# Order of two first loads on the ACT queue, and the length of TensorE's fillers, in a gated attention and mixer kernel

## The chip, the cores and the metric

The kernel runs on one core of a Trainium2 chip. The metric is the device time of one execution in microseconds (us). Medians are of all executions of a kernel, and runs count as "fast" where nothing put them over 1.5% above the fastest of the same kernel. The whole kernel takes about 267 us, and the change is about the first 7 of them, so everything below is about tenths of a microsecond.

## The reference

```python
def reference(A_x, A_wqkv, A_wo, B_x, B_w1, B_w2, B_w3, B_w4, gate_w):
    x = A_x                                            # 1 x 2048 x 640, bf16
    g = sigmoid((x * gate_w).sum(-1, keepdims=True))   # one gate per row
    a = A_ref(x, A_wqkv, A_wo)                         # linear attention, 32 heads
    b = B_ref(x, B_w1, B_w2, B_w3, B_w4)               # mixer block and MLP
    return g * a + (1 - g) * b
# A_ref begins with qkv = x @ wqkv; the kernel starts with the k part of it.
# ... the rest is not touched by the change
```

## The kernel before

It starts with k = x @ wk, for 16 chunks of 128 rows. The product needs x transposed. Chunk 0 is loaded as it is (`load_x(0, 1)`), transposed by TensorE against an identity matrix and copied from PSUM by VectorE. The other chunks come through loads that transpose (`load_xT`), all on the sync queue. The 640 x 640 matrix wk comes in five pieces of 128 rows (`load_wk`), of 160 KB each. The gate vector is transposed too and becomes one more column of wk, so that the gate's logits fall out of the same products.

```python
    sp, aq, gq = nc.sync, nc.scalar, nc.gpsimd
    # load_x, load_xT: on sp.  load_wk(q, dc): rows dc*128 to dc*128+127 of wk, on queue q
    load_x(0, 1)
    aq.dma_start(g5[:], gate_w.rearrange("(c p) -> c p", p=P))
    load_wk(sp, 1)
    load_wk(aq, 0)
    load_wk(aq, 2)
    load_wk(sp, 3)
    load_wk(aq, 4)
    for c0, c1 in ((1, 2), (2, 3), (3, 4), (4, 6), (6, 8), (8, 12), (12, 16)):
        load_xT(c0, c1)
    # ... the other loads
    def warmup(n, w=TS):                      # TS = 512: fillers, their result is never read
        for i in range(n):
            nc.tensor.matmul(warm[:, 1, 0:w], lhsT=one[:, 0:P], rhs=one[:, 0:w], start=True, stop=True)

    warmup(6)
    warmup(3, P)                              # P = 128
    # ... tiles
    for n, (ptb, a, b) in enumerate(turns):   # ((0, 2), (2, 5)): five transposes in two groups
        for dc in range(a, b):
            nc.tensor.transpose(ptb[...], x_sb[:, 0, dc * P:(dc + 1) * P], ident[:])
        nc.vector.tensor_copy(xT[:, a:b, 0:P], ptb[...])
        if n == 0:
            nc.tensor.transpose(tg[:, 0:DC], g5[:], ident[0:DC, 0:DC])
            nc.vector.tensor_copy(wk_sb[:, :, D], tg[:, 0:DC])
    warmup(3, P)
    for dc in range(DC):                      # chunk 0, piece by piece as wk lands
        k_mm(kp, 0, (dc,))
        if dc < DC - 1:
            warmup(1, 2 * P)
    k_evac(kp, 0)
    for c in range(1, NCH):                   # chunks 1 to 15
        pt = pair()
        k_mm(pt, c, range(DC))
        k_evac(pt, c)
```

Of the kernel before, what the change touches and what calls it, by code (L numbers as in the profile page):

```python
# [16 lines left out]
def kernel(  # L17
# [14 lines left out]
    P = 128  # L32
# [36 lines left out]
    def pair():  # L69
        return ps.tile([P, 2, 512], F32, name="pp")  # L70
# [44 lines left out]
    sp, aq, gq = nc.sync, nc.scalar, nc.gpsimd  # L115

    def load_x(c0, c1):
        sp.dma_start(x_sb[:, c0:c1, 0:D], x2[c0 * P:c1 * P, :].rearrange("(c p) d -> p c d", p=P))
# [4 lines left out]
    def load_wk(q, dc):  # L123
        q.dma_start(wk_sb[:, dc, 0:D], A_wqkv[dc * P:(dc + 1) * P, D:2 * D])  # L124

    load_x(0, 1)
    aq.dma_start(g5[:], gate_w.rearrange("(c p) -> c p", p=P))
    load_wk(sp, 1)
    load_wk(aq, 0)
    load_wk(aq, 2)  # L130
    load_wk(sp, 3)
    load_wk(aq, 4)
# [67 lines left out]
    def warmup(n, w=TS):  # L200
        for i in range(n):
            nc.tensor.matmul(warm[:, 1, 0:w], lhsT=one[:, 0:P], rhs=one[:, 0:w], start=True, stop=True)

    warmup(6)
    warmup(3, P)
    kp = pair()
    turns = [(pair()[:, 0, :].bitcast(BF16), a, b) for a, b in ((0, 2), (2, DC))]
    tg = warm[:, 0, :].bitcast(BF16)
# [387 lines left out]
```

## Time and profile before

| | before |
|---|---|
| median | 266.91 us of 3 (266.3, 266.91 and one of 305.26) |
| span of the profiled execution | 264.4 us |
| TensorE busy | 259.7 us, 98% |
| first x chunk lands | 3.08 us |
| transposes start | 3.66 us |
| first product with wk | 4.73 us |
| chunk 1 starts | 6.57 us |
| transposed chunks 8 to 11 land | 16.29 us |
| chunk 8 starts | 16.34 us |

Times in such tables are counted from the span's start. Landings and starts of single matmuls come from the trace. L190 is the line of the k products, L202 of the fillers, L211 and L214 of the transposes, L121 of the transposing loads, L118 of plain x loads, L124 of the wk pieces.

Busy times of the kernel before, from the page: engine, us, share of the span, instructions.

```profile
PE 259.7 (98%) x1744; PEld 162.2 (61%) x1744; DVE 139.3 (53%) x270; ACT 85.1 (32%) x126; POOL 20.2 (8%) x55
```

TensorE bounds the kernel as a whole. But the chain of waits of the first 30 us of the kernel before (start us, us, what) does not run through TensorE until 16.3 us:

```profile
0.79 0.40 SPq L118
...
2.18 1.29 SPq L121
...
3.52 1.27 SPq L121
...
9.35 6.94 DMA xT<-in_A_x_dram
16.29 0.05 issue
16.34 11.07 PE pp L190 x80
```

SPq is the sync queue, which issues one load after another; a transposing load holds it for over 1.2 us. The sixth one, of chunks 8 to 11, is issued at 9.35 us and lands 6.94 us later. TensorE begins chunk 8 only then.

The k products of the kernel before, and what TensorE's weight loads waited for (us, times):

```profile
L190 PE MATMUL pp<-wk_sb,xT x160: 296/300/310, 4.7 to 27.1; 128*128 128x320 bf16 x80, 128*128 128x321 bf16 x80
...
  DMA xT<-in_A_x_dram: 0.6, 2
```

The three numbers are the least, median and greatest duration in ns: no product is slow. A chunk takes ten of them, 1.36 us. With chunk 1 at 6.57 us and no wait, chunk 8 would start at 6.57 + 9.54 = 16.11 us (9.54 is the distance of these two starts when TensorE doesn't wait). It started at 16.34, so about 0.23 us were spent waiting. That is the slack behind the start.

TensorE in the start of the kernel before, from the timeline (start us, us, engine, line, operation):

```profile
2.92 0.95 PE L202 MATMUL pp<-const-bfloat16-1.0 128*128 128x512 bf16 x4
3.66 0.42 PE L211 MATMUL pp<-ident,x_sb 128*128 128x128 bf16 x2
4.01 0.18 PE L214 MATMUL pp<-ident,g 5*128 5x5 bf16 x1
4.13 0.36 PE L211 MATMUL pp<-ident,x_sb 128*128 128x128 bf16 x3
4.55 0.33 PE L202 MATMUL pp<-const-bfloat16-1.0 128*128 128x128 bf16 x3
4.73 0.43 PE L190 MATMUL pp<-wk_sb,xT 128*128 128x320 bf16 x2
```

The first x load and its time to landing, kernel before:

```profile
L118 SPq DMA_DIRECT2D x_sb<-in_A_x_dram x1: 402/402/402, 0.8 to 0.8; - x1
...
DMA to landing us min/median/max: 2.3/2.3/2.3
```

Piece 0 of wk, second on the ACT queue, landed at 4.68 us and its first product started at 4.73. So piece 0 looks like what held chunk 0 back. But the last of the three short fillers ahead of that product began at 4.67 us, 0.06 us before it, so this trace alone can't tell whether chunk 0 waited for the piece or for TensorE itself.

### The profile page before, as it was taken

The page shows a single profiled execution, that of the slowest core. Times are in us where ns is not written, and L with a number is a line of the kernel's source. Part 1 is how long each engine was busy: PE and PEld are TensorE (multiplying, and loading weights), DVE is VectorE, ACT ScalarE, POOL GpSimd, SP SyncE. Part 2 cuts the span into 40 slices and gives each one's busy share as a digit, 9 for nine tenths or more (in the row PEclk, how much of TensorE's full clock was granted, in tenths as well). Part 3 has the DMA queues.
Part 4 walks back from the last instruction along what each step waited for, and adds up shares of the span by engine and source line. Part 5 has one row for each costly group of instructions (what it writes and reads, how often), then busy time and mean ns, then how long its engine had stood idle before and what let it go on. Part 6 is the DMA issues. An engine that isn't in the chain of part 4 may idle for free.

```text
span 264.4 us, 4255 instructions
## 1 busy us (share of the span) xinstructions
PE 259.7 (98%) x1744; PEld 162.2 (61%) x1744; DVE 139.3 (53%) x270; ACT 85.1 (32%) x126; POOL 20.2 (8%) x55
## 2 busy tenths in 40 slices
PE   8999999999999999999999999999999999999994
PEld 4767555788755644555667555667565667455762
DVE  1788688899858588955403464503455313112132
ACT  1555444321165636622502212312131422233000
POOL 7100010012300140001000001000001000000000
PEclk9999999999999999999999999999999999999999
DMA  7999978015673727600132000042000041100011
GB/s 202 184 211 365 377 222 318 0 43 121 128 92 68 78 51 193 207 0 2 25 74 77 25 0 2 0 99 75 26 0 2 1 99 58 44 0 2 0 59 40
DMA packets 46093, 23.61 MB, mean 89 GB/s; under 512 B 35451, under 2 KB 45435, under 8 KB 46075
## 3 DMA queue, kind: packets, MB, share of 16 engines
q1 hardware_dynamic: 45632, 22.86, 34.0%
q10 hardware_dynamic: 442, 0.49, 0.5%
q8 instruction: 13, 0.21, 0.3%
q14 instruction: 6, 0.04, 0.1%
HBM read 12.21 MB, written 2.62 MB: 56 GB/s over the span
## 4 chain that ended last, share of the span: by engine, by line
PE 91%; SPq 3%; DMA 3%; ACT 1%; issue 0%; DVE 0%
PE pp L479 22%; PE pp L460 21%; PE pp L307 8%; PE pp L413 8%; PE pp L444 8%; PE pp L341 8%; PE pp L232 8%; PE pp L190 4%; SPq L121 3%; DMA xT<-in_A_x_dram 3%; PE pp L468 1%; PE pp L488 1%; ACT m_sb L381 1%; PE pp L360 1%; PE pp L247 0%; SPq L124 0%
## 5 line engine op out<-in xcount | busy, mean ns | idle before, releaser
L460 PE MATMUL pp<-lnxT,w_sb 128*128 128x512 bf16 x260 | 60.4, 379 | 0.0
L479 PE MATMUL pp<-w_sb,h 128*128 128x256 bf16 (+1 forms) x416 | 57.9, 299 | 0.0
L462 ACT ACTIVATE h<-pp 128x1024 bf16<-128x1024 f32 (+1 forms) x28 | 26.9, 961 | 82.2 <-PE pp L460 82.2
L479 PEld LDWEIGHTS <-h 128*128 128x128 bf16 x416 | 40.3, 98 | 16.6 <-issue 1.1
L460 PEld LDWEIGHTS <-w_sb 128*128 128x128 bf16 x260 | 25.4, 98 | 26.8
L495 DVE SCALAR_TENSOR_TENSOR oc<-pp,omg,x 128x640 bf16<-128x640 f32 x15 | 12.9, 882 | 44.0 <-ACT h2x L471 21.3
L447 DVE SCALAR_TENSOR_TENSOR x<-pp,gate,x 128x640 f32<-128x640 f32 x16 | 13.9, 868 | 29.4 <-PE pp L444 29.4
L416 DVE TENSOR_TENSOR x<-pp,x_sb 128x640 f32<-128x640 f32 x16 | 13.1, 820 | 22.6 <-PE pp L413 22.6
L182 ACT ACTIVATE e<-pp 128x640 bf16<-128x640 f32 (+1 forms) x26 | 21.5, 826 | 9.6 <-PE pp L232 9.6
L444 PE MATMUL pp<-m_sb,pqT 128*128 128x320 bf16 x160 | 24.3, 299 | 0.0
L413 PE MATMUL pp<-w_sb,hsT 128*128 128x320 bf16 x160 | 23.9, 299 | 0.1
L190 PE MATMUL pp<-wk_sb,xT 128*128 128x320 bf16 (+1 forms) x160 | 22.6, 300 | 0.1
L307 PE MATMUL pp<-x_sb,pk 128*128 128x320 bf16 (+1 forms) x160 | 22.3, 300 | 0.0
L232 PE MATMUL pp<-xT,hsT 128*128 128x512 bf16 x100 | 21.7, 379 | 0.0
L307 PEld LDWEIGHTS <-pk 128*128 128x128 bf16 x160 | 18.8, 117 | 3.5
L413 PEld LDWEIGHTS <-hsT 128*128 128x128 bf16 x160 | 15.6, 98 | 8.2 <-issue 0.2
L444 PEld LDWEIGHTS <-pqT 128*128 128x128 bf16 x160 | 15.7, 98 | 7.7
L190 PEld LDWEIGHTS <-xT 128*128 128x128 bf16 x160 | 15.4, 98 | 6.4 <-DMA xT<-in_A_x_dram 0.6
L341 PE MATMUL pp<-lnxT,w_sb 128*128 128x512 bf16 x80 | 17.9, 379 | 0.0
L232 PEld LDWEIGHTS <-hsT 128*128 128x128 bf16 x100 | 11.8, 118 | 9.7
L277 POOL TENSOR_SCALAR rstd<-mv 128x4 f32<-128x4 f32 (+1 forms) x11 | 3.4, 313 | 156.5 <-DVE mv L283 156.5
L184 DVE SCALAR_TENSOR_TENSOR pk<-pp,e 128x640 bf16<-128x640 f32 x16 | 13.2, 825 | 1.7
(77 smaller groups left out, 191.6 us busy)
## 6 DMA issues: line engine op xcount, KB each, us to landing
out_dram<-oc SPq DMA_DIRECT2D x15, 160.0 KB, 1.8
w_sb<-in_B_w_dram SPq DMA_DIRECT2D x1, 2160.0 KB, 8.4
w_sb<-in_B_w_dram SPq DMA_DIRECT2D x1, 2080.0 KB, 10.0
x_sb<-in_A_x_dram SPq DMA_DIRECT2D x2, 640.0 KB, 10.7
x_sb<-in_A_x_dram SPq DMA_DIRECT2D x1, 1120.0 KB, 8.2
wo_sb<-in_A_wo_dram SPq DMA_DIRECT2D x6, 160.0 KB, 8.3
hsT<-in_A_wqkv_dram SPq DMA_DIRECT2D x1, 800.0 KB, 5.7
m_sb<-in_A_wqkv_dram SPq DMA_DIRECT2D x1, 800.0 KB, 11.5
```

The costliest lines, as they stand in the source:

```text
L182: nc.scalar.activation(ev, src, ACT.Exp)
L184: nc.vector.scalar_tensor_tensor(dst, src, 0.0, ev, op0=ALU.max, op1=ALU.add)
L190: nc.tensor.matmul(pt[:, hf, 0:n], lhsT=xT[:, dc, c * P:(c + 1) * P], rhs=wk_sb[:, dc, hf * HD:hf * HD + n], start=(dc == 0), stop=(dc == ...
L232: nc.tensor.matmul(pt[:, t % 2, :], lhsT=wq_sb[:, dc, :].rearrange("p (m j) -> p j m", j=DC)[:, j], rhs=xT[:, dc, t * TS:(t + 1) * TS], st ...
L307: nc.tensor.matmul(pt[:, hf, 0:HD + hf], lhsT=w, rhs=x_sb[:, c, hf * HD:(hf + 1) * HD + hf], start=(c == 0), stop=(c == NCH - 1))
L341: nc.tensor.matmul(pt[:, i, :], lhsT=w, rhs=lnxT[t][:, dc, :], start=(dc == 0), stop=(dc == DC - 1))
L413: nc.tensor.matmul(pt[:, hf, 0:HD], lhsT=hsT[:, fc, 2 + c * P:2 + (c + 1) * P], rhs=w2_sb[:, fc, hf * HD:(hf + 1) * HD], start=(fc == 0), ...
L444: nc.tensor.matmul(pt[:, hf, 0:HD], lhsT=pqT[:, j, c * P:(c + 1) * P], rhs=m_sb[:, j, hf * HD:(hf + 1) * HD], start=(j == 0), stop=(j == D ...
L447: nc.vector.scalar_tensor_tensor(x1, pt[:, :, 0:HD], gate[:, c:c + 1], x1, op0=ALU.mult, op1=ALU.add)
L460: nc.tensor.matmul(pt[:, k, :], lhsT=w3_sb[:, dc, fc * P:(fc + 1) * P], rhs=lnT[:, dc, :], start=(dc == 0), stop=(dc == DC - 1))
L462: nc.scalar.activation(h2[:, 2 * i * TS:(2 * i + n) * TS], pt[:].rearrange("p h e -> p (h e)")[:, 0:n * TS], ACT.Gelu_apprx_tanh)
L479: nc.tensor.matmul(dst, lhsT=st[t]["h2"][:, fc * TS + cc * P:fc * TS + (cc + 1) * P], rhs=w4_sb[:, fc, a:b], start=start and fc == 0, stop ...
```

## The change

Its intent: piece 0 is wanted first of all pieces, so it goes first on its queue, and the gate vector second. The fillers are lengthened to keep TensorE at work until x is there.

```diff
     load_x(0, 1)
+    load_wk(aq, 0)
+    load_wk(sp, 1)
     aq.dma_start(g5[:], gate_w.rearrange("(c p) -> c p", p=P))
-    load_wk(sp, 1)
-    load_wk(aq, 0)
     load_wk(aq, 2)
@@
-    warmup(6)
-    warmup(3, P)
+    warmup(7)
+    warmup(1, P)
```

One more thing moves that the diff doesn't show. Eight semaphores serve the loads of the sync and ACT queues in turn (numbers 100 and 102 to 108 in the traces of both kernels). The second transposing load shares its semaphore with the first load on the ACT queue: the gate vector before, piece 0 after.

## The prediction

> **What bounds the kernel now.** TensorE: the busy table gives PE 259.7 us of a 264.4 us span (98%). The change touches only the first 7 us, and there the chain of waits does not run through PE: from 0.79 to 16.29 us it follows the sync queue, which issues the first x load, two wk pieces and then seven transposing loads of x, one after another at 1.27 to 3.56 us each. It leaves that queue with the landing of transposed chunks 8 to 11 at 16.29 us; PE takes over at 16.34. Reading the matmuls one by one, chunk 7 has streamed out by about 16.12, so PE stands still some 0.22 us there: the slack behind the start.
>
> **The start, from the timeline.** Six 512-wide fillers run from 0.83 us, 0.427 us apart [...]; three 128-wide ones (0.107 us each) end at 3.66. The first x chunk landed at 3.08, so its transposes begin only when the fillers end. The gate vector, first on the ACT queue (0.57 us to issue), landed at 2.14, long before its use at 4.01. Wk piece 0, second there, landed at 4.68, and its first product started at 4.73, just as the last short filler ended. Chunk 0 runs to 6.54 us; chunk 1 starts at 6.57, when its transposed x has landed (6.52).
>
> **What the change does.** It removes two 128-wide fillers and adds one 512-wide: 0.427 - 0.213 = +0.21 us ahead of the transposes, which begin near 3.88. Wk piece 0 is issued at 0.79 instead of 1.39, so it should land 0.6 to 1 us earlier, near 3.7 to 4.1. It now starts beside the first x load. [...] I expect x to land near 3.4 to 3.9 (this trace shows x alone, 2.3 us to landing, the other pieces at 3.3 to 3.9). The gate vector lands near 2.6 to 4, perhaps just in time. So chunk 0 starts at about 4.9 and ends near 6.7.
>
> **A side effect.** The second transposing load on the sync queue waits for the semaphore of the first DMA on the ACT queue. That was the gate vector's (2.14; no wait, the load was issued at 3.52). Now it is wk piece 0's. If that lands after 3.5, the transposing loads, which are on the chain, slip by 0 to 0.5 us; I guess 0.2.
>
> **On the critical path.** PE being 0.15 to 0.2 us later at the start is swallowed by the 0.22 us wait at chunk 8. An earlier wk piece 0 buys nothing there either. The slip of the transposing loads would pass on in full. Sum: 0 to +0.5 us, middle +0.1 us, of 266.9.
>
> **Prediction:** 267.0 us, 8 in 10 between 266.1 and 268.0. Faster by over 2%: 0.01; within 2%: 0.97; slower by over 2%: 0.02.
>
> **What would show it.** Right: the chain of waits still enters PE at chunk 8, near 16.3 to 16.6 us, behind the transposing load; wk piece 0 lands before 4.2; x lands after 3.3; later stages keep their lengths. Wrong: chunk 8 starts below 16.2, or PE waits for x or the gate vector for over 0.3 us.
>
> **What would make it wrong.** The full clock was granted at 4.2 us[...]. A faster landing of the transposing loads could gain up to 0.2 us, as much as PE waits for them.

Three passages are cut from the text, and the cuts are marked, because no trace or run shows what they said: a word on the clock of the fillers (the trace has no clock record before 4.2 us), a reason for the later landing of x, and the length and cost of a later full clock. None was a term of the sum, which came to 0 to +0.5 us, middle +0.1 us, on 266.9 us: the later clock was named as a risk beside it.

## The result, and the profile after

The changed kernel took 266.87 us in the median of 4 executions (266.47 to 266.91). The kernel before stood at 266.7 us in the median of 4 by then, one of them the 305.26. The ratio of the fast runs was 1.0008, with a 95% interval of 0.9988 to 1.0028: the same. Ratios here are the mean time of one kernel's fast runs over that of the other's of the same rounds, so not quite the ratio of the medians quoted.

The first trace after the change looks quite different from the one before, for a change of nothing. Busy times of the changed kernel, from the page:

```profile
PE 260.5 (98%) x1743; PEld 162.8 (61%) x1743; DVE 139.3 (53%) x270; ACT 85.1 (32%) x126; POOL 20.3 (8%) x55
```

Its chain of waits in the first 30 us:

```profile
0.83 3.25 PE pp L202 x8
...
5.24 0.54 PE pp L190 x2
...
6.66 0.27 PE pp L190 x2
...
7.42 20.71 PE pp L190 x152
```

Here the chain is TensorE from the first filler on. The same pair of k products takes 0.54 us at 5.24 and 0.27 us at 6.66: at 5.24 us TensorE took twice as long for the same work. The trace's clock records begin with the full clock at 6.445 us, against 4.205 us in the trace before. The k products say the same, and that nothing was waited for (the list of waits is empty):

```profile
L190 PE MATMUL pp<-wk_sb,xT x160: 299/300/475, 5.0 to 27.8; 128*128 128x320 bf16 x80, 128*128 128x321 bf16 x80
```

TensorE in the start, from the timeline of the changed kernel:

```profile
3.88 0.42 PE L211 MATMUL pp<-ident,x_sb 128*128 128x128 bf16 x2
4.23 0.18 PE L214 MATMUL pp<-ident,g 5*128 5x5 bf16 x1
4.34 0.50 PE L211 MATMUL pp<-ident,x_sb 128*128 128x128 bf16 x3
4.76 0.48 PE L202 MATMUL pp<-const-bfloat16-1.0 128*128 128x128 bf16 x3
5.04 0.74 PE L190 MATMUL pp<-wk_sb,xT 128*128 128x320 bf16 x2
```

And the first x load of the changed kernel:

```profile
L118 SPq DMA_DIRECT2D x_sb<-in_A_x_dram x1: 397/397/397, 0.8 to 0.8; - x1
...
DMA to landing us min/median/max: 2.8/2.8/2.8
```

Piece 0 did land earlier: at 3.77 us instead of 4.68. But x landed later, at 3.60 instead of 3.08, and chunk 0 began at 5.04 us instead of 4.73. Chunk 1 began at 7.53 instead of 6.57, chunk 8 at 17.07 instead of 16.34, and the span grew from 264.43 to 265.16 us: 0.73 us, the same 0.73 as at chunk 8. All that follows chunk 8 kept its length.

The clock wasn't the only thing that came late. The first transposing load, which brings chunk 1, was issued at 2.18 us in both traces and landed at 6.52 us before, 7.28 after. Its time to landing, first in the kernel before, then in the changed one:

```profile
DMA to landing us min/median/max: 4.3/4.3/4.3
DMA to landing us min/median/max: 5.1/5.1/5.1
```

In the kernel before, chunk 1 started 0.05 us after this landing. With an early clock, chunk 1 of the changed kernel could therefore not have started before about 7.33 us, and chunk 8 not before 7.33 + 9.54 = 16.87 us. By this estimate some 0.5 of the 0.73 us would have remained in this trace without the late clock.

One might stop here and say that the change costs 0.7 us. Two traces can't carry that: the timed executions of the two kernels spread over 0.6 us (before) and 0.4 us (changed), and the traced execution of the kernel before took 266.17 us, less than any of its timed ones.

### The profile page after: what moved, and what is told of

The parts are those of the page before. It is cut to its first block, busy times and chain, and to the rows that moved or that the text cites. A ratio compares the mean times of both kernels' runs of the same rounds, so it can differ in the third digit from the quotient of the medians.

```text
span 265.2 us, 4253 instructions
## 1 busy us (share of the span) xinstructions
PE 260.5 (98%) x1743; PEld 162.8 (61%) x1743; DVE 139.3 (53%) x270; ACT 85.1 (32%) x126; POOL 20.3 (8%) x55
## 4 chain that ended last, share of the span: by engine, by line
PE 97%; ACT 1%; DVE 0%; issue 0%
PE pp L479 22%; PE pp L460 21%; PE pp L190 8%; PE pp L307 8%; PE pp L413 8%; PE pp L444 8%; PE pp L341 8%; PE pp L232 8%; PE pp L202 2%; PE pp L468 1%; PE pp L488 1%; ACT m_sb L381 1%; PE pp L360 1%; PE pp L247 0%; PE pp L379 0%; PE pp L211 0%
## 5 line engine op out<-in xcount | busy, mean ns | idle before, releaser
L479 PEld LDWEIGHTS <-h 128*128 128x128 bf16 x416 | 40.3, 98 | 16.6 <-issue 1.1
```

Source lines behind the costliest of these rows:

```text
L479: nc.tensor.matmul(dst, lhsT=st[t]["h2"][:, fc * TS + cc * P:fc * TS + (cc + 1) * P], rhs=w4_sb[:, fc, a:b], start=start and fc == 0, stop ...
```

## The experiments

Theory A: the difference of the two traces is chance, above all the time at which TensorE gets its full clock; the change itself does nothing. Theory B: the change costs time, through the loads or through the fillers. All runs below gave correct results.

### Both kernels again

No edit. The first kernel is the one before:

> The kernel before, unchanged, profiled and timed against itself. Theory A (the time by which the full clock is granted to TensorE falls by chance in each execution, and this alone makes the 0.7 us difference of the two first traces): executions spread over 266.2 to 266.9 us, ratio 1.000 within 0.001; [...]the span follows it: near 264.4 us for a grant by about 4.2 us, near 265.2 us for one past 6 us. Theory B (the change itself makes the difference): the grant is again at 4.2 us, the span again 264.4 us, the executions sit near 266.2 to 266.5 us.

Measured: 266.57 us median of 6 (266.14 to 267.17), ratio 1.0 (0.9988 to 1.0012). The full clock came at 5.35 us instead of 4.21, and the span was 264.88 us instead of 264.43: with no edit at all. Chunk 8 waited again, as chunks 8 to 11 landed at 16.74 us instead of 16.29 and its first product started at 16.78. (The profile's chain puts part of that wait down to a ScalarE copy that had just ended; the landing 46 ns ahead of the start is the one that fits, as it does in all four traces with this wait.)

The changed kernel again:

> The changed kernel, unchanged. Theory A: executions spread over 266.2 to 266.9 us as those of the kernel before do, ratio 1.000 within 0.0015; the grant falls elsewhere than 6.4 us in this trace or, if it falls late, PE again waits for nothing at chunk 8. Theory B: ratio 1.001 to 1.003, grant again past 6 us, span again 265.2 us. Wk piece 0 lands again at 3.6 to 4.1 us, and the second transposing load is again issued 0.2 to 0.5 us later than the 3.52 us of the kernel before.

Measured: 266.96 us median of 5 (266.64 to 266.97), ratio 1.0011 (0.9999 to 1.0023). Its chain of waits:

```profile
0.79 3.14 DMA wk_sb<-in_A_wqkv_dram
3.92 0.02 issue
3.94 1.20 SPq L121
...
9.75 7.38 DMA xT<-in_A_x_dram
17.12 0.05 issue
17.17 2.90 PE pp L190 x20
```

Its k products and waits:

```profile
L190 PE MATMUL pp<-wk_sb,xT x160: 296/300/309, 5.1 to 27.9; 128*128 128x320 bf16 x80, 128*128 128x321 bf16 x80
...
  DMA xT<-in_A_x_dram: 1.4, 3
```

The full clock came at 4.08 us this time, earlier than in any trace of the kernel before, and no product was slow. Yet the span was 265.24 us, as long as with the late clock. The load path made it so: chunk 1 started at 7.03 us, right after its x had landed (6.97), and from there TensorE would have reached chunk 8 at 16.56 us, but chunks 8 to 11 landed only at 17.12. That is 0.83 us later than in the first trace of the kernel before: 0.39 us from the later issue (9.75 instead of 9.35) and 0.44 us because the load took longer (7.38 instead of 6.94). The first lines show the side effect of the shared semaphore. The second transposing load started at 3.94 us, right after piece 0 had landed (3.92), where the kernel before has 3.52. And x landed only at 4.12 us, so that the transposes started at 4.16, after the fillers had ended.

So theory A fails as an account of all of it: the full clock came at other times with no edit (4.21 and 5.35 us in the kernel before, 6.45 and 4.08 in the changed one), but an early clock didn't bring the changed kernel's time down. What holds in both traces is that the start of chunk 8 is the later of two arrivals, TensorE's own and the landing of chunks 8 to 11. And in every trace of a fast execution, those below included, the span is this start plus 247.9 to 248.1 us.

### The order of the loads alone

```diff
     load_x(0, 1)
+    load_wk(aq, 0)
+    load_wk(sp, 1)
     aq.dma_start(g5[:], gate_w...)
-    load_wk(sp, 1)
-    load_wk(aq, 0)
```

> Only the order of the two loads on the ACT queue, with the old fillers. Both theories: x lands near 3.6 us instead of 3.08, wk piece 0 near 3.8 instead of 4.68, the second transposing load is issued near 3.8 instead of 3.52. The old fillers end at 3.66, so PE loses at most 0.05 us waiting for x. Theory A: ratio 1.000 within 0.001. Theory B, if the loads are to blame: 1.001 to 1.003.

Measured: 266.73 us median of 5, ratio 1.0004 (0.9992 to 1.0016). x landed at 3.70 us, piece 0 at 3.92, the second transposing load started at 3.94, the transposes at 3.75 and chunk 0 at 4.88 us. Everything expected of the loads came, though TensorE lost 0.08 us before the transposes instead of at most 0.05. In the time it can't be told from nothing.

### The fillers alone

```diff
-    warmup(6)
-    warmup(3, P)
+    warmup(7)
+    warmup(1, P)
```

> Only the fillers (7 wide and 1 short), with the old load order. Transposes start at 3.88 instead of 3.66, x lands at 3.08, gate vector at 2.1, wk piece 0 at 4.7, second transposing load at 3.52. With an early grant the 0.2 us are swallowed by the wait of 0.22 us for chunks 8 to 11 near 16.3 us. Theory A: ratio 1.000 within 0.001. Theory B, if the fillers are to blame: 1.001 to 1.003 and a late grant.

Measured: 266.43 us median of 5, ratio 0.9995 (0.9983 to 1.0007). The traced execution had a late clock (6.63 us) and was the slowest of the five, 266.94 us; its chunk 8 started at 17.16 us without any wait. x landed at 3.05 us and the second transposing load started at 3.53. The transposes started at 3.88 us and chunk 0 at 5.04, both as in the first trace of the changed kernel, where x had landed at 3.60: so it was the fillers, and not the late x, that moved the start of chunk 0 there. Longer fillers alone don't cost time that can be seen. A late clock in this trace says little for theory B: two kernels with the old fillers had one still later (6.72 and 6.66 us, below).

### The gate vector on the GpSimd queue

```diff
-    aq.dma_start(g5[:], gate_w...)
+    gq.dma_start(g5[:], gate_w...)
```

in the changed kernel, so that piece 0 is first on its queue but no longer shares a semaphore with the second transposing load.

> The changed kernel, but the gate vector goes to the GpSimd queue. Then the semaphore that the second transposing load waits for is no longer that of wk piece 0. If the late start of that load comes from this shared semaphore, it is issued at 3.5 us (3.78 and 3.94 with the change, 3.52 before), and the later ones 0.2 to 0.3 us earlier too; if it came from the DMA engines being busy, it stays near 3.8. x still lands near 3.6 to 4.1 us beside wk piece 0. Time: if the slip of the transposing loads is what costs, ratio near 0.9995 to 1.0005 (after_again: 1.0011).

Measured: 266.86 us median of 6, two of them 268.61 and 268.94; ratio 1.0033 (1.0005 to 1.006). The second transposing load started at 3.53 us, with x landing at 3.77 and piece 0 at 3.96 us, beside each other as in the changed kernel. Its line in this trace, with its duration in ns and its start in us:

```profile
L121 SPq DMA_TRANSPOSE xT<-in_A_x_dram x1: 1267/1267/1267, 3.5 to 3.5; - x1
```

So its late start does come from the shared semaphore and not from busy DMA engines. The traces with the sharing agree: in after, after_again, order_only and split_after it was issued 16 to 17 ns after piece 0 had landed. But the trade was bad, for another reason. A wait of this kernel (engine, line, what it waited for, us in total, times, longest):

```profile
PE pp L214 <- DMA g<-in_gate_w_dram: 0.9, 1, 0.9
```

The gate vector now came too late, and chunk 0 began at 5.69 us. The time expected (0.9995 to 1.0005) was missed.

### Cutting the transposing load of chunks 8 to 11

```diff
-    for c0, c1 in ((1, 2), (2, 3), (3, 4), (4, 6), (6, 8), (8, 12), (12, 16)):
+    for c0, c1 in ((1, 2), (2, 3), (3, 4), (4, 6), (6, 8), (8, 10), (10, 12), (12, 16)):
```

If chunk 8 is where two arrivals meet, then landing chunks 8 and 9 earlier leaves TensorE's own path alone. First in the kernel before:

> The kernel before, with the transposing load of chunks 8 to 11 cut in two (8, 9 and 10, 11). Theory (the start is the later of two arrivals at chunk 8: PE's own, or the landing of the transposed chunks 8 to 11): chunks 8 and 9 now land near 14.5 us, PE never waits there, chunk 8 starts at PE's own time (16.1 us with a full clock by 4.2 us, up to about 17.0 with one past 6 us), and the span is that plus 248.08 us. Ratio 0.9985 to 1.000. Rival (the wait at chunk 8 only moves to chunk 10 or 12): ratio 1.000 or above, chunk 12 starts no earlier than 21.8 us.

Measured: 266.19 us median of 6, five between 266.13 and 266.38 and one of 268.21, so that the ratio is 0.9999 (0.9977 to 1.0021). Chunks 8 and 9 landed at 14.11 us, chunk 8 started at 16.68 us without a wait, and nothing was waited for at chunk 12. The outlier blurred the ratio, so it was run again:

> split_before once more, for the outlier and for a second trace. Median 266.1 to 266.3 us against 266.6 us before; chunk 8 starts at chunk 1's start + 9.55 us, with no wait; span that + 248.08 us.

Measured: 266.3 us median of 6 (265.87 to 266.76), ratio 0.9988 (0.9976 to 0.9999). Its k products; the list of what they waited for is empty:

```profile
L190 PE MATMUL pp<-wk_sb,xT x160: 299/300/300, 4.8 to 26.9; 128*128 128x320 bf16 x80, 128*128 128x321 bf16 x80
```

With the full clock by 4.77 us, chunk 1 started at 6.605 us and chunk 8 at 16.142, 9.537 us later; the span was 264.13 us, the shortest of all traces. The wait of 0.2 us at chunk 8 was real, and it is gone.

Then the same cut in the changed kernel:

> The changed kernel with the same cut. PE's own path alone decides now, so it should be slower than split_before by the longer fillers and the later x: 0.2 to 0.3 us, ratio to the kernel before 0.9995 to 1.001. If the slip of the transposing loads were the only cost, it would equal split_before within 0.05 us for the same grant of the clock.

Measured: 266.62 us median of 5 (266.52 to 267.08), ratio 1.0009 (0.9996 to 1.0022). x landed at 4.08 us and the transposes started at 4.13 us, where both traces of the cut kernel with the old order have 3.66. The mean of the five is 266.76 us. The mean of the cut kernel before, of 11 executions without the 268.21, is 266.27 us, so the change costs about 0.49 us here; the scatter of the executions gives this difference a standard error of 0.14. With the outlier kept, which counts as fast by the rule above, it is 0.33 us with a standard error of 0.21, which can't be told from nothing. The 11 executions also come from two sessions on two chips; the medians of the one session that had both kernels are 266.62 and 266.19 us. So with the wait at chunk 8 gone, the changed kernel is likely slower, by about as much as the 0.2 to 0.3 us expected or somewhat more.

What made it slower isn't shown. In the trace of split_after the late x is not what came last: the third load on the ACT queue, piece 2, landed at 6.18 us and its product waited for it, and chunk 1 started at 7.30 us, 0.05 us after its own x had landed (7.26). In split_before piece 2, at 6.06 us, held TensorE too, for 0.46 us, with the full clock from 4.56 us; chunk 1 started at 7.14.

### The slip of the transposing loads, made larger

```diff
     for n, (c0, c1) in enumerate(((1, 2), (2, 3), ...)):
         load_xT(c0, c1)
+        if n == 0:
+            for k in range(2):
+                sp.dma_start(idle[:, k, :], gate_w...)   # 1.2 KB, never read
```

in the kernel before.

> The kernel before, with two loads of 1.2 KB (the gate vector once more, into a tile that nothing reads) between the first and the second transposing load on the sync queue: their start slips by about 1.1 to 1.2 us and almost no bytes are added. This doubles and doubles again the slip of 0.26 to 0.42 us that the changed order brought. If the slip passes on to the landing of chunks 8 to 11 and so to the end, that landing moves from 16.2 to 16.7 to about 17.3 to 17.9 us, chunk 8 starts right behind it, and the time rises by 0.7 to 1.1 us: ratio 1.0025 to 1.004. If the DMA engines have room to catch up, the landing stays below 16.9 and the ratio below 1.0012.

Measured: 267.03 us median of 6 (266.5 to 267.78), ratio 1.0015 (1.0002 to 1.0029). The second transposing load started at 4.64 us, 1.12 us later than before. Not all of that is the time to issue the two loads, which ended at 4.34 us: they also moved the semaphores on, so that the second transposing load shared one with piece 0 and waited for its landing, as in the changed kernel. The mean rose by 0.4 us (0.0015 of 266.6), with 0.05 to 0.8 us inside the interval. So less than the whole slip reached the end, about a third by the mean; neither of the two ratios expected (1.0025 to 1.004, or below 1.0012) was met, but the interval reaches into both. Its chain of waits shows that the meeting point moved:

```profile
1.39 3.24 DMA wk_sb<-in_A_wqkv_dram
...
4.64 1.21 SPq L121
...
7.21 4.16 DMA xT<-in_A_x_dram
11.38 0.05 issue
11.42 8.62 PE pp L194 x62
```

(L194 is the k product's line in this kernel.) TensorE waited at chunk 4, whose load landed at 11.38 us, and not at chunk 8. The load of chunks 8 to 11 was issued at 10.25 us, 0.89 us later than before, but landed at 16.25: 6.0 us after its issue instead of 6.94. This trace is of the fastest of the six executions (266.5 us), so it doesn't show where the 0.4 us of the mean came from.

### One issue less on the sync queue

```diff
-    load_wk(sp, 3)
+    load_wk(aq, 3)
```

in the kernel before.

> The kernel before, with wk piece 3 moved from the sync queue to the ACT queue. The transposing loads are issued 0.46 us earlier (first 1.72, second about 3.05). If their issue sets the landing of chunks 8 to 11, that falls from 16.2 to 16.7 us to about 15.8 to 16.3, chunk 8 starts at PE's own time in most executions, ratio 0.999 to 0.9997. If the DMA engines set the landing, it stays at 16.2 to 16.7 and the ratio at 1.000.

Measured: 267.16 us median of 6 (266.34 to 268.13), ratio 1.0022 (1.0004 to 1.0041). The load of chunks 8 to 11 was issued at 8.82 us and landed at 15.12, so an earlier issue does bring an earlier landing in the trace. The time didn't follow: with a clock that came at 6.72 us, TensorE reached chunk 1 at 7.55 us and never waited at chunk 8. That one late clock doesn't explain a slower median; what does, stays open.

### Piece 0 earlier without a load beside x

```diff
-    load_wk(sp, 1)
-    load_wk(aq, 0)
+    load_wk(sp, 0)
+    load_wk(aq, 1)
```

with the cut of above, in the kernel before.

> The cut kernel, with wk pieces 0 and 1 exchanged between the queues: piece 0 goes second on the sync queue behind x, piece 1 second on the ACT queue behind the gate vector. This gives what the change wanted without a load beside x: x still lands at 3.05 us, piece 0 at 4.2 instead of 4.4 to 4.7, chunk 0 starts at 4.72, when the fillers end. Time as split_again, within 0.0005 of its ratio.

Measured: 266.45 us median of 6 (265.87 to 266.88), ratio 0.9987 (0.9975 to 1.0), as split_again's 0.9988. In the traced execution x landed at 3.38 us and piece 0 at 4.99: the gain for piece 0 was not seen. The clock came at 6.66 us, with the old fillers.

Last, the same without the three short fillers:

```diff
     warmup(6)
-    warmup(3, P)
```

> As split_swap, without the three short fillers ahead of the transposes: they begin at about 3.4 instead of 3.66, chunk 0 at about 4.45. Where chunk 1 waits for its transposed x (6.5 to 7.0 us) or chunk 0 for its last wk pieces (5.9 to 6.5), nothing is won; where the clock comes late, up to 0.25 us. Ratio to split_swap 0.999 to 1.000.

Measured: 266.22 us median of 6: four between 266.07 and 266.3, one of 268.34, and one of 392.52 us, with a granted clock of 0.659, which is the one that was traced. The ratio of the fast runs is 0.9998 (0.9972 to 1.0024). To split_swap's mean, that of the five fast ones stands as 1.0007, outside the 0.999 to 1.000 expected, and without the 268.34 as 0.9990, inside. No trace of a fast execution shows where the time came from. The one trace may be used for its start alone: x landed at 3.05 us and piece 0 at 4.05, so the gain for piece 0 that split_swap's trace lacked was there, and the transposes began at 3.34 us and chunk 0 at 4.50.

### What the traces have in common

| kernel | full clock from, us | x lands | second transposing load issued | chunk 1's x lands | chunk 1 starts | chunks 8 (to 11) land | chunk 8 starts | span |
|---|---|---|---|---|---|---|---|---|
| before | 4.21 | 3.08 | 3.52 | 6.52 | 6.57 | 16.29 | 16.34 | 264.43 |
| before_again | 5.35 | 3.05 | 3.52 | 6.60 | 6.89 | 16.74 | 16.78 | 264.88 |
| after | 6.45 | 3.60 | 3.78 | 7.28 | 7.53 | 16.13 | 17.07 | 265.16 |
| after_again | 4.08 | 4.12 | 3.94 | 6.97 | 7.03 | 17.12 | 17.17 | 265.24 |
| order_only | 5.34 | 3.70 | 3.94 | 6.69 | 6.91 | 16.55 | 16.59 | 264.68 |
| filler_only | 6.63 | 3.05 | 3.53 | 6.61 | 7.62 | 16.20 | 17.16 | 265.22 |
| split_before | 4.56 | 3.01 | 3.53 | 7.01 | 7.14 | 14.11 | 16.68 | 264.66 |
| split_again | 4.77 | 3.01 | 3.52 | 6.52 | 6.61 | 13.87 | 16.14 | 264.13 |
| split_after | 5.19 | 4.08 | 3.91 | 7.26 | 7.30 | 14.31 | 16.85 | 264.86 |

In each row chunk 8 starts either some 0.046 us after its load landed, or 9.54 us after chunk 1 (9.55 in split_after).

Chunk 1 in turn starts 0.05 us after its own x landed in before, after_again and split_after, and later than that in the other rows, where TensorE came later by its own work, the clock or piece 2. In three of the four rows with the new load order its x landed at 6.97 to 7.28 us, and in four of the five with the old order at 6.52 to 6.61. But order_only has 6.69, split_before 7.01, and split_swap and slip_twice, with the old place of the gate vector, 7.06 and 6.82. Whether the change delays this load isn't settled.

Was piece 0 what held chunk 0 back, as it seemed at first? No. In split_before, which loads it as the kernel before does, piece 0 landed at 4.41 us instead of 4.68, and chunk 0 started at the same time, 4.72 instead of 4.73 us, right behind the fillers. In before_again piece 0 had landed at 4.35 us and chunk 0 started at 4.82, before the full clock came (5.35). Only in split_swap, where piece 0 landed at 4.99 us, did chunk 0 start behind it (5.04).

## Why the prediction was right or wrong

The time was right: 267.0 us predicted, 266.87 measured, within 266.1 to 268.0. "Within 2%" was right. But this says little for the mechanism: the range holds every timed execution of both kernels but the slow one of 305.26 us, so a guess of "no change" would have been right as well. Of the signs that the prediction named for itself, piece 0 before 4.2 us, x after 3.3 us and later stages of the same length came in both traces. The main one did not: chunk 8 was to start near 16.3 to 16.6 us behind its load, and it started at 17.07 us without a wait in one trace and at 17.17 us behind its load in the other. In both the start was some 0.7 to 0.8 us later than in the first trace of the kernel before, in two different ways. That the median still came out within 0.1% is in part luck: the 266.9 us that the prediction started from, a median of three with the slow one among them, lies 0.3 us above the mean of the 36 fast executions of the kernel before that are counted below (266.61), while the loss of the changed kernel was more likely 0.2 us than 0.1. The steps:

- **TensorE bounds the kernel; the start is governed by the sync queue's transposing loads.** Right for the trace it was read from. It isn't a fixed property of the kernel. The landing of chunks 8 to 11 scattered from 16.20 to 16.74 us in before, before_again and filler_only, which have the old load order, and TensorE's own arrival from about 16.1 to 17.2 us with the clock. Which of the two ends the wait differs from execution to execution.
- **Transposes near 3.88 us, piece 0 landing near 3.7 to 4.1.** Right: 3.88 us in the first trace and 3.77 and 3.92 for piece 0. In the second the transposes began at 4.16 us, since x landed late.
- **x landing near 3.4 to 3.9 because piece 0 is beside it.** Right in kind and once too low: 3.60 and 4.12 us (3.70 and 4.08 in the kernels order_only and split_after). x has the transposes, the PSUM copy and more fillers behind it before the first product, 3.66 to 4.73 us in the kernel before; piece 0 has nothing. So a landing of piece 0 0.4 to 0.9 us earlier gained nothing, and x paid for it with one 0.5 to 1.1 us later. Chunk 0 started at 5.04 and 5.09 us instead of 4.73 and 4.82. The late x explains that in the second trace alone: there the fillers had ended by 3.88 us and the transposes waited until 4.16. In the first, x was there at 3.60 us, and the longer fillers held the transposes until 3.88, as in filler_only.
- **Chunk 0 at 4.9 us, ended near 6.7.** Too early by 0.15 to 0.2 us at its start. Its end was off by more. In the first trace chunk 1 started at 7.53 us instead of 6.57: TensorE was 0.96 us late, not 0.15 to 0.2, as the clock came at 6.45 us and chunk 1's x, too, only at 7.28. In the second chunk 1 started at 7.03 us, behind its x. The prediction has no term for a later landing of this load. The gate vector landed at 3.74 and 4.02 us, within the 2.6 to 4 predicted or just past it, and wasn't waited for.
- **"PE being 0.15 to 0.2 us later at the start is swallowed by the 0.22 us wait at chunk 8."** Not so in the first trace: there TensorE's delay was larger than the slack and came out at the end as 0.73 us. With the cut load, where no wait at chunk 8 is left, the changed kernel was slower by about 0.3 to 0.5 us, which with the outlier kept isn't clear of the scatter. filler_only, where the delay alone was added to the old load order, didn't get slower, as the step said.
- **The side effect: the second transposing load slips by 0 to 0.5 us, guess 0.2.** Right: 0.26 and 0.42 us, and gate_pool shows that the shared semaphore is the cause.
- **"The slip of the transposing loads would pass on in full."** Not as a rule. With the change itself, the load of chunks 8 to 11 was issued 0.30 us later and landed 0.16 us earlier in the first trace (9.65 and 16.13 us), and was issued 0.39 us later and landed 0.83 us later in the second. A slip of 1.12 us, made on purpose, cost about 0.4 us of time (0.05 to 0.8). The landing itself varies by more than the slip: 6.0 to 7.5 us after issue over the uncut kernels.
- **A late clock as the risk.** The prediction named it; how much later it would come and what that would cost is cut from the text above, as no trace was behind this estimate of the author's. The risk was the right one, but it wasn't rare and wasn't the change's doing. The full clock came anywhere from 3.91 to 6.72 us, with old and new fillers alike. filler_only (6.63 us) and wk3_on_act (6.72 us), with the old place of piece 0, started chunk 1 at 7.62 and 7.55 us instead of the 6.57 of the first trace of the kernel before (4.21 us), and their spans are 0.8 and 0.7 us longer. The fillers began at 0.83 us in every trace, wherever the full clock then came. What sets its time isn't shown.

Is there any true effect of the change? Both measurements of the changed kernel say "the same", and both intervals hold 1 (1.0008 and 1.0011). All 9 executions of the changed kernel together have a mean of 266.84 us. The 36 fast ones of the kernel before that ran beside the experiments and in the first measurement have 266.61 us. The difference of 0.23 us, 0.09%, has a standard error of 0.07 from the scatter of the executions, though chips differed between sessions, which it doesn't count. A small loss is likely, then, but its division between the later x of chunk 0 and of chunk 1, longer fillers and the slip isn't settled: order_only and filler_only, each alone, can't be told from nothing.

Open also: the executions at 267.4 to 268.9 us (one to three of six) of gate_pool, split_before, wk3_on_act, slip_twice and split_swap_short, which neither the kernel before nor the changed one showed; the executions at 305 and 392 us; and why a load of the same chunks takes 6.0 to 7.5 us to land.

The version that the experiments point to is the kernel before with the load of chunks 8 to 11 cut in two: ratio 0.9988 (0.9976 to 0.9999) in the run without an outlier, 0.9999 with one. That is a gain of about 0.3 us in the first and none in the second; all 12 executions together (0.18 us below the kernel before, standard error 0.18) don't tell it from nothing.

## What to carry to other kernels

Of two loads that are wanted at the start, look at what follows each landing, and not at which wait ended last in one trace: here the load with work behind it, x, landed 0.5 to 1.1 us later for having a second one of its size beside it (2.8 to 3.3 us after its issue, and 2.2 to 2.3 in most traces with the gate vector there, 2.6 in split_swap), and the other one's earlier landing gained nothing. Before reordering loads, look up which semaphore each later load waits for: here piece 0, moved to the front of its queue, became what an unrelated load waited for, and that load started at 3.78 and 3.94 us instead of 3.52, and at 3.53 when the sharing was undone (gate_pool). Where two arrivals meet with 0.2 us between them, profile the unchanged kernel twice before believing a difference of 0.7 us between two traces.
